# Moving the softmax divisor's small steps from VectorE to ScalarE in a top-k attention and expert kernel

## The chip, the cores and the metric

The kernel runs on one core of a Trainium2 chip. The metric is the device time of one execution in microseconds (us); lower is better. The core has five engines with a queue each, and each queue is worked off in order: TensorE (PE; its weight loads are listed as PEld), VectorE (DVE), ScalarE (ACT), GpSimd (POOL) and SyncE (SP, which here only issues transfers). They meet through semaphores alone.

## The reference

Two blocks follow each other. All data are float32.

```python
# attention: B, H, S, D = 8, 8, 576, 64
scores = q @ k.T / sqrt(D)
kth    = the 32nd largest score of each row
scores = where(scores >= kth, scores, -1e9)
attn   = exp(scores - rowmax)
attn   = attn / (attn.sum(-1) + 1e-09)
x      = (attn @ v) rearranged to (B*S, H*D)          # 4608 x 512
# experts: E = 8, F = 1024
logits = x @ w_gate; e = argmax(logits)
y      = relu(x @ w1[e]) @ w2[e]                      # each row by its own expert
out    = softmax(logits)[e] * y
```

What the change is about is the third last line of the attention block: the row sum of the exponentials, plus 1e-09, by which a row is divided. The kernel multiplies by its reciprocal instead, and does so late, on the finished rows of `x`.

## The kernel before, in words

Two heads of one batch make a *unit*, so there are 32 units (8 batches of 4). A unit has 1152 score rows of 576 keys: nine tiles of 128 rows, four for each head and one shared tail of 64 rows from each. Two tiles are worked on together; nine such pairs cover two neighbouring units, so the main loop `loop()` has 144 passes. In each block of nine passes, pass 0 to 3 belong to the even unit, pass 4 holds the tails of both, and 5 to 8 belong to the odd unit.

One pass goes through the engines like this. TensorE makes the scores (line 276), three passes ahead. ScalarE copies them to SBUF (line 283, tile `s`). VectorE searches each row's 32nd largest score: `fold` (lines 290, 292) and `fold_on` (298, 300) halve the rows, then come rounds of MAX8 (329, 338) and MATCH_REPLACE8 (345). ScalarE scales the threshold (354, tile `low`) and makes a mask by two Relus (370). GpSimd subtracts the mask (379). ScalarE takes the exponentials (387), whose accumulator gives the row sums: one column of the tile `z` (128 x 9, one per unit) for each tile of rows. TensorE transposes the weights (398, 409, 411), ScalarE copies them out of PSUM (402, 404, 417, 419).

When a unit's tiles are done, its end runs in slices spread over later passes. `ending` is a generator that yields the name of the *place* in the pass at which its next slice goes: "small" (behind the search), "relu" (behind the Relus), "products" (at the end of the pass), "rows". The slices are: products with `v` (432), a copy `oT` (434), the second half of both, a turn back with the gate's logits (443), a copy `xl` (450), then GpSimd's scaling by the reciprocals in `logits` (466) and `rows` (479). The reciprocals lie in `rz`, 128 x 10: nine columns as in `z`, and a tenth whose first 64 partitions hold the second head's tail, moved there from partitions 64 to 127 of the ninth. There are two `rz`, for even and odd units.

`divisors` (lines 452 to 459) makes `rz`. It is a generator of VectorE steps, put on the list `aside`; `tick()` takes one step of that list after each MAX8 and MATCH_REPLACE8 of the search from its second round on. So the three small instructions (454 adds epsilon, 456 takes the reciprocal, 458 moves the tenth column) stand between the MAX8s of the next pass's search, in this order: MAX8 (338), 454, MAX8, 456, MATCH_REPLACE8, 458, MATCH_REPLACE8.

The order of instructions on PE, ACT and DVE is that of the program (`manual_schedule`). From the sixth block on, slices of the expert block (`pieces`: lines 663 to 717) are put between, in numbers that the program fixes in advance. What is left of the experts runs after the attention, on TensorE with ScalarE copying out.

Of the kernel before, what the change touches and what calls it, by code (L numbers as in the profile page):

```python
# [11 lines left out]
AF = mybir.ActivationFunctionType  # L12
# [9 lines left out]
EPS = 1e-9  # L22
# [13 lines left out]
def kernel(  # L36
# [46 lines left out]
    nc = tc.nc  # L83
    B, U, P, _ = qk.shape
# [7 lines left out]
    ST = S - SM  # L92
# [5 lines left out]
    NT = 2 * NC + 1  # L98
# [91 lines left out]
    def token_ids(t, b):  # L190
        return nc.gpsimd.iota(t, pattern=[[P, KC]], base=b * S, channel_multiplier=1)

    oT_of, rz_of = [], []
    for n in range(2):
        t = const.tile([P, S if n else KC * P], F32, name=f"oT{n}")
        if not n:
            nc.gpsimd.memset(t[:, S:], 0.0)
        oT_of.append(t)
        t = const.tile([P, NT + 1], F32, name=f"rz{n}")
        nc.gpsimd.memset(t, 0.0)  # L200
        rz_of.append(t)
    wT = const.tile([P, NC, 2, S + ST], F32, name="wT")
    wTt = const.tile([P, S + ST], F32, name="wTt")
# [30 lines left out]
    def in_turn(put):  # L234

        if not k.exact:
            tc.keep_in_program_order(put)
        return put
# [4 lines left out]
    def load_values(n):  # L243
        n.v = k.load.tile([P, KC, P], F32, name="vb")
        nc.sync.dma_start(n.v, v[n.b, n.u, :, :].rearrange("(c p) d -> p c d", p=P))
# [65 lines left out]
    def through(steps):  # L311
        for _ in steps:
            pass
        if steps in aside:
            aside.remove(steps)
# [105 lines left out]
    def outputs(n, x):  # L421

        odd = n.u % 2
        oT = oT_of[odd]
        for j in range(2):
            q = slice(j * HF + (0 if odd else ST), (j + 1) * HF + (0 if odd else ST))
            po = bank("po")
            for c in range(KC):
                for h in range(2):
                    r = slice(h * D, (h + 1) * D)  # L430
                    rhs = wT[:, c, h, q] if c < NC else wTt[:, q]
                    nc.tensor.matmul(po[r, 0:HF], n.v[:, c, r], rhs, start=(c == 0), stop=(c == KC - 1))  # L432
            yield
            nc.scalar.copy(oT[:, j * HF:(j + 1) * HF], po[:, 0:HF])
            yield
        starts = [t * P + (ST if odd else 0) for t in range(NC)] + [0 if odd else SM]
        xw = P + lw
        n.xl = k.small.tile([P, KC, xw], F32, name="xl", bufs=1)
        put = []
        for t0, t1 in ((0, KC - 2), (KC - 2, KC)):  # L440
            px = bank("px")
            for t in range(t0, t1):
                nc.tensor.matmul(
                    px[:, (t - t0) * xw:(t - t0 + 1) * xw], oT[:, starts[t]:starts[t] + P],
                    turn[:, n.u // 2, odd * lw:odd * lw + xw], start=True, stop=True,
                )
            put.append((n.xl[:, t0:t1, :], px[:, 0:(t1 - t0) * xw].rearrange("p (t w) -> p t w", w=xw)))
        yield
        for to, px in put:
            nc.scalar.copy(to, px)  # L450

    def divisors(n):
        rz = rz_of[n.u % 2]
        nc.vector.tensor_scalar_add(rz[:, 0:NT], n.z, EPS)
        yield
        nc.vector.reciprocal(rz[:, 0:NT], rz[:, 0:NT])
        yield
        nc.vector.tensor_copy(rz[0:ST, NT:NT + 1], rz[ST:P, NT - 1:NT])
        yield

    def logits(n, lg):

        rzb = rz_of[n.u % 2][:, :].rearrange("p (t h) -> p t h", h=2)
        at = P if n.u % 2 else 0
        lt = n.xl[:, :, at:at + lw].rearrange("p t (h e) -> p t h e", h=2)
        in_turn(nc.gpsimd.tensor_tensor(lt, lt, _inner(rzb, E), op=ALU.mult))
        if n.u:
            in_turn(nc.gpsimd.tensor_tensor(lg, lg, lt[:, :, 0, :], op=ALU.add))
            in_turn(nc.gpsimd.tensor_tensor(lg, lg, lt[:, :, 1, :], op=ALU.add))
        else:  # L470
            in_turn(nc.gpsimd.tensor_tensor(lg, lt[:, :, 0, :], lt[:, :, 1, :], op=ALU.add))

    def rows(n, x):

        rzb = rz_of[n.u % 2][:, :].rearrange("p (t h) -> p t h", h=2)
        at = 0 if n.u % 2 else lw
        xu = x[:, :, n.u * P:(n.u + 1) * P].rearrange("p t (h d) -> p t h d", h=2)
        xl = n.xl[:, :, at:at + P].rearrange("p t (h d) -> p t h d", h=2)
        in_turn(nc.gpsimd.tensor_tensor(xu, xl, _inner(rzb, D), op=ALU.mult))
# [25 lines left out]
    def ranks(r):  # L505

        rp = bank("rank")
        ohf = r.oh[:, :, :].rearrange("p t e -> p (t e)")
        r.pos, r.run = rp[:, 0:KC * E], rp[:, KC * E:(KC + 1) * E]
        nc.tensor.matmul(rp[:, 0:(KC + 1) * E], ident, _ins(run[:, :], 1, KC + 1), start=True, stop=False)  # L510
        nc.tensor.matmul(r.pos, before, ohf, start=False, stop=False)
        for i in range(1, KC + 1):
            nc.tensor.matmul(
                rp[:, i * E:(KC + 1) * E], ones, ohf[:, 0:(KC + 1 - i) * E], start=False, stop=(i == KC)
            )
# [219 lines left out]
    with fast:  # L735
# [68 lines left out]
        def ending(b, u):  # L804

            nonlocal left
            n = unit[b * U + u]
            if u == 0:
                x_of[b] = k.xp.tile([P, KC, XW], F32, name="x")
                in_turn(token_ids(x_of[b][:, :, Dm + 1].bitcast(I32), b))  # L810
                lg_of[b] = k.small.tile([P, KC, E], F32, name="lg")
            x, lg = x_of[b], lg_of[b]
            out_steps = outputs(n, x)
            yield "products"
            next(out_steps)
            if u % 2 == 0:
                yield "relu"
                next(out_steps)
            yield "small"
            div = divisors(n)  # L820
            aside.append(div)
            if u % 2:
                yield "relu"
                next(out_steps)
            yield "products"
            next(out_steps)
            if b * U + u + 2 < len(units):
                load_values(unit[b * U + u + 2])
            yield "relu"
            next(out_steps)  # L830
            yield "products"
            next(out_steps)
            yield "relu"
            next(out_steps, None)
            yield "rows"
            through(div)
            logits(n, lg)
            rows(n, x)
            if u < U - 1:
                return  # L840
            yield "small"
            r = choice(lg)
            aside.append(r.steps)
            yield "weights"
            yield "turn"
            through(r.steps)
            nc.scalar.activation(lg, lg, AF.Exp)
            yield "products"
            ranks(r)
            yield "small"  # L850
            steps = places(r, x)
            aside.append(steps)
            yield "relu"
            nc.scalar.copy(run, r.run)
            yield "pool"
            through(steps)
            scatters.extend(scattering(r, x))
            if b == B - 1:
                scatter(KC)
                slot_i = k.small.tile([1, 2, NSLOT], I32, name="slot_i")  # L860
                through(table(slot_i, SURE, False))
                firsts = [(slot_i[0:1, 0, j:j + 1], slot_i[0:1, 1, j:j + 1]) for j in range(SURE)]
                ready = load_rows(SimpleNamespace(), firsts[0][1], True)
            new = LAST - SURE if b == B - 1 else new_of[b]
            if new:
                slot_i = slot_last if b == B - 1 else k.small.tile([1, 2, NSLOT], I32, name="slot_i")
                steps = table(slot_i, new, b == B - 1)
                aside.append(steps)
                yield "weights"
                yield "pool"  # L870
                yield "weights"
                yield "pool"
                through(steps)
                coming.extend((slot_i[0:1, 0, j:j + 1], slot_i[0:1, 1, j:j + 1]) for j in range(new))
            if b == B - 1:
                spare.extend(coming[ALWAYS - SURE:])
                del coming[ALWAYS - SURE:]
                assert len(loaded) == 2 and not waiting
                fill_up()
                coming[0:0] = [(firsts[0][0], ready)] + [(expert, (piece,)) for expert, piece in firsts[1:]]  # L880
                scatter(0)
# [125 lines left out]
    with ExitStack() as outer:  # L1007
# [10 lines left out]
        with ExitStack() as st:  # L1018
# [7 lines left out]
            with tc.For_i(0, B, 1) as b:  # L1026
# [3 lines left out]
                for u in range(0, U, 2):  # L1030
# [4 lines left out]
                    for g in groups(u):  # L1035
# [10 lines left out]
                        n, tile = tiles[0]  # L1046
# [76 lines left out]
```

## Time and profile before

| | |
|---|---|
| median of 4 runs | 1374.2 us (1374.14 to 1376.15) |
| the profiled execution, its own time | 1377.23 us |
| its span, first to last instruction | 1375.5 us |
| TensorE clock granted, mean | 0.948 |
| PE busy | 1236.3 us (90%), 7666 instructions |
| DVE busy | 1094.4 us (80%), 4655 |
| ACT busy | 919.7 us (67%), 2049 |
| POOL busy | 647.7 us (47%), 805 |

The busy share is taken over the whole span, which has two stages: the attention with some expert slices up to about 1100 us, in which all four engines work, and the rest of the experts, in which VectorE has almost nothing to do. In the profile a row of the groups names line, engine, operation, tiles and shapes, the count, then busy time and mean duration, then the idle time of that engine just before. A wait is written "engine tile line <- who ended it: us in total, times, longest".

### The profile page before, as it was taken

Reading aid. Unit: us, or ns where it says so; the run is one execution under the profiler, and the core shown is the slowest. Engines: PE = TensorE matmul, PEld = TensorE weight load, DVE = VectorE, ACT = ScalarE, POOL = GpSimd, SP = SyncE. Lnnn points to the kernel's source line nnn. Section 1 sums busy time; section 2 is a strip of 40 time slices with the busy share of each in tenths; the row PEclk is TensorE's granted clock in tenths of the full one; section 3 lists DMA queues with packets and bytes.
Section 4 is the critical chain, followed back from the end, with each engine's and each line's share of the span. In section 5 each row is a group of like instructions: output and inputs, shape, how many; then the busy total and the mean of one; then the engine's idle time right before and its main releaser. Section 6 shows DMA issues by size and latency. Waiting matters only on the chain. (4 is left out here: it accounts for less than half of the span.)

```text
span 1375.5 us, 24487 instructions
## 1 busy us (share of the span) xinstructions
PE 1236.3 (90%) x7666; PEld 839.7 (61%) x7666; DVE 1094.4 (80%) x4655; ACT 919.7 (67%) x2049; POOL 647.7 (47%) x805
## 2 busy tenths in 40 slices
PE   5676777677799999999999999999999999999995
PEld 3344444444466666666766666767676667776773
DVE  8999999999999999999999999999999820000000
ACT  4787778878788888888777788887777821111110
POOL 3454557546645565466555655575556521000000
PEclk9888778788899999999999999999999999999998
DMA  2000011001473357326644474358542759999880
GB/s 82 29 29 29 28 36 55 29 29 36 156 287 137 112 200 289 130 82 241 255 167 174 154 278 154 113 178 304 181 167 83 299 181 356 388 319 333 301 322 18
DMA packets 102220, 231.68 MB, mean 168 GB/s; under 512 B 5182, under 2 KB 25918, under 8 KB 102080
## 3 DMA queue, kind: packets, MB, share of 16 engines
q1 hardware_dynamic: 95328, 209.76, 42.9%
q0 software_dynamic: 6464, 19.97, 4.0%
q8 instruction: 62, 1.02, 0.3%
q14 instruction: 78, 0.64, 0.1%
q10 hardware_dynamic: 288, 0.30, 0.1%
HBM read 208.72 MB, written 22.33 MB: 168 GB/s over the span
## 5 line engine op out<-in xcount | busy, mean ns | idle before, releaser
L379 POOL TENSOR_TENSOR w<-s,w 128x576 f32<-128x576 f32 x288 | 407.3, 1434 | 450.1 <-ACT w L370 449.8
L688 PE MATMUL ph<-xTs,w 128*128 128x128 f32 x2560 | 308.5, 276 | 6.0 <-ACT xTs L665 6.0
L688 PEld LDWEIGHTS ph<-xTs,w 128*128 128x128 f32 x2560 | 297.5, 192 | 26.2 <-issue 18.9
L703 PE MATMUL py<-w,hT 128*128 128x512 f32 x640 | 292.2, 596 | 0.0
L338 DVE MAX8 tops<-scr 128x8 f32<-128x168 f32 x864 | 248.6, 320 | 0.1
L276 PE MATMUL sc<-qkb 64*128 64x288 f32 (+1 forms) x1280 | 222.0, 472 | 9.4 <-ACT s L283 5.2
L387 ACT ACTIVATE w<-w,nbias 128x576 f32<-128x576 f32 x288 | 224.7, 798 | 2.2 <-POOL w L379 2.0
L370 ACT ACTIVATE w<-s,low 128x576 f32<-128x576 f32 x288 | 207.7, 768 | 4.7
L398 PE MATMUL wTm<-turn,w 128*128 128x128 f32 x1152 | 172.9, 291 | 37.8 <-ACT xl L450 25.5
L398 PEld LDWEIGHTS wTm<-turn,w 128*128 128x128 f32 x1152 | 134.7, 148 | 98.5 <-issue 35.4
L1002 DVE CAST any_i<-pd 1x1 int32<-1x1 f32 x1 | 0.1, 147 | 236.0 <-PE pd L1000 236.0
L703 PEld LDWEIGHTS py<-w,hT 128*128 128x128 f32 x640 | 114.4, 190 | 117.6 <-issue 116.5
L345 DVE MATCH_REPLACE8 scr<-tops,scr 128x168 f32<-128x168 f32 x576 | 178.1, 314 | 0.0
L283 ACT COPY s<-sc 128x576 f32<-128x576 f32 x288 | 169.9, 645 | 11.7 <-PE sc L276 11.1
L404 ACT COPY wT<-wTm 128x512 f32<-128x512 f32 x256 | 140.0, 609 | 39.2 <-PE wTm L398 39.0
L276 PEld LDWEIGHTS sc<-qkb 64*128 64x128 f32 (+1 forms) x1280 | 118.3, 195 | 72.8 <-issue 26.4
L432 PE MATMUL po<-wT,vb 128*64 128x288 f32 x1024 | 158.5, 458 | 0.4 <-ACT wTt L419 0.4
L709 POOL DMA_INDIRECT out_dram<-y,xg x40 | 40.6, 1014 | 211.9 <-ACT y L717 199.3
L329 DVE MAX8 few<-l 128x8 f32<-128x288 f32 x288 | 128.0, 445 | 0.0
L432 PEld LDWEIGHTS po<-wT,vb 128*64 128x64 f32 x1024 | 75.5, 152 | 78.6 <-issue 31.1
L693 ACT ACTIVATE hT<-ph 128x512 f32<-128x512 f32 x80 | 48.7, 609 | 108.6 <-PE ph L688 108.5
L290 DVE TENSOR_TENSOR h<-s 128x576 f32<-128x576 f32 x144 | 115.3, 801 | 3.9 <-ACT s L283 3.9
(116 smaller groups left out, 1429.2 us busy)
## 6 DMA issues: line engine op xcount, KB each, us to landing
w<-in_moe_w_dram SPq DMA_DIRECT2D x80, 2048.0 KB, 9.6
qkb<-in_qk_dram SPq DMA_DIRECT2D x31, 608.0 KB, 4.1
xg<-x_rows SPq DMA_DIRECT2D x40, 257.0 KB, 9.8
vb<-in_v_dram SPq DMA_DIRECT2D x32, 320.0 KB, 3.2
x_rows<-blank SPq DMA_DIRECT2D x5, 257.0 KB, 14.2
x_rows<-blank POOLq DMA_DIRECT2D x4, 257.0 KB, 8.7
x_rows<-x,posi POOLq DMA_INDIRECT x40, 3.1
out_dram<-y,xg POOLq DMA_INDIRECT x40, 6.1
```

The source lines that it names most:

```text
L276: nc.tensor.matmul(ps[rows, j, 0:HF], n.q[d, cols], n.k[d, keys], start=True, stop=True)
L283: lambda m=m, ps=ps: nc.scalar.copy(s[:, m, :, :], ps[:, :, 0:HF]) for m, ps in enumerate(got)
L338: nc.vector.max(out=tops[:, m, r * 8:(r + 1) * 8], in_=src[m])
L345: nc.vector.match_replace(out=scr[:, m, :], in_to_replace=tops[:, m, r * 8:(r + 1) * 8], in_values=src[m], imm_value=NEG,)
L370: nc.scalar.activation(w[:, m, :], s[:, m, :, :].rearrange("p j k -> p (j k)"), AF.Relu, scale=-STEEP, bias=low[:, m:m + 1],)
L379: k.last_pool = in_turn(nc.gpsimd.tensor_tensor(w[:, m, :], s[:, m, :, :].rearrange("p j k -> p (j k)"), w[:, m, :], op=ALU.subtract)).ins
L387: nc.scalar.activation(w[:, m, :], w[:, m, :], AF.Exp, scale=scale, bias=nbias[:, m:m + 1], accum_out=n.z[:, c:c + 1])
L398: nc.tensor.transpose(pm[:, c * P:(c + 1) * P], w[:, m, first:first + P], ident)
L404: nc.scalar.copy(wT[:, :, m, q], pm4)
L432: nc.tensor.matmul(po[r, 0:HF], n.v[:, c, r], rhs, start=(c == 0), stop=(c == KC - 1))
L688: nc.tensor.matmul(ph[:, f, :], n.w1[:, 0, dt, fc * P:(fc + 1) * P], n.xT[:, dt, :], start=(dt == 0), stop=(dt == DT - 1),)
L703: nc.tensor.matmul(py, hT[:, f, :], n.w2[:, 0, f, :], start=(f == 0), stop=(f == FT - 1))
```

## The change

`divisors` now gives ScalarE the sum with epsilon and the shifted tenth column, as two activations (a Copy with a constant bias), and VectorE one reciprocal over ten columns. The two activations are issued at once at the place "relu", behind the Relus of the pass (for odd units behind the copy `oT` too, for even units one pass after it); only the reciprocal stays on `aside`. The order of `ending` is changed to fit, and `rz` begins as ones, since the reciprocal now also reads the tenth column's other 64 partitions. On each of the other engines the order of instructions is as before, and so is that of all other instructions on these two.

```diff
-        nc.gpsimd.memset(t, 0.0)
+        nc.gpsimd.memset(t, 1.0)
         rz_of.append(t)
...
     def divisors(n):
         rz = rz_of[n.u % 2]
-        nc.vector.tensor_scalar_add(rz[:, 0:NT], n.z, EPS)
+        nc.scalar.activation(rz[:, 0:NT], n.z, AF.Copy, bias=EPS)
+        nc.scalar.activation(rz[0:ST, NT:NT + 1], n.z[ST:P, NT - 1:NT], AF.Copy, bias=EPS)
         yield
-        nc.vector.reciprocal(rz[:, 0:NT], rz[:, 0:NT])
-        yield
-        nc.vector.tensor_copy(rz[0:ST, NT:NT + 1], rz[ST:P, NT - 1:NT])
+        nc.vector.reciprocal(rz[:, 0:NT + 1], rz[:, 0:NT + 1])
         yield
...
             yield "products"
             next(out_steps)
+            yield "relu"
+            next(out_steps)
             if u % 2 == 0:
                 yield "relu"
-                next(out_steps)
-            yield "small"
             div = divisors(n)
+            next(div)
             aside.append(div)
-            if u % 2:
-                yield "relu"
-                next(out_steps)
             yield "products"
             next(out_steps)
```

## Prediction

> **What bounds the kernel now.** I read the 40 slices of the page first, then the groups with shapes kept apart, the waits, and the timeline around the lines of the change.
>
> ```profile
> PE   5676777677799999999999999999999999999995
> DVE  8999999999999999999999999999999820000000
> ACT  4787778878788888888777788887777821111110
> ```
>
> For 32 slices VectorE is full. TensorE joins it from the twelfth slice and carries the rest alone. So until about 1100 us two engines could be the bound; who waits for whom decides.
>
> ```profile
> DVE h L290 <- ACT s L283: 3.9, 4, 1.3
> ACT low L354 <- DVE tops L338: 87.3, 71, 4.2
> ```
>
> VectorE waited for scores 4 times in 144 passes, 3.9 us in all. ScalarE waited for VectorE's thresholds 71 times, 87.3 us. VectorE sets the pace, and ScalarE, with TensorE behind it, follows. By stretches the second wait is 65.0 us before 400 us, 14.7 us from 400 to 640, none from 640 to 760, 6.9 us from 760 to 920, none from 920 to 1040. In the two stretches with none VectorE itself waited 1.3 us each for scores: there the followers are the bound.
>
> The groups of the change, and two of ScalarE's as prices (busy us, mean ns):
>
> ```profile
> L454 DVE TENSOR_SCALAR rz<-z 128x9 f32<-128x9 f32 x32 | 15.7, 490 | 0.8 <-ACT w L387 0.8
> L456 DVE RECIPROCAL rz<-rz 128x9 f32<-128x9 f32 x32 | 6.2, 193 | 0.0
> L458 DVE COPY rz<-rz 64x1 f32<-64x1 f32 x32 | 4.8, 149 | 0.9
> L354 ACT ACTIVATE low<-tops 128x2 f32<-128x2 f32 x144 | 31.4, 218 | 87.7 <-DVE tops L338 87.3
> L854 ACT COPY run<-rank 128x8 f32<-128x8 f32 x8 | 1.2, 154 | 2.6 <-PE rank L513 2.6
> ```
>
> The sum with epsilon is dear for nine columns: 490 ns in the mean. The view of line 454 gives its spread, and the timeline of unit 19 (units counted from 0) the reason:
>
> ```profile
> L454 DVE TENSOR_SCALAR rz<-z x32: 151/174/1410, 56.8 to 1101.7; 128x9 f32<-128x9 f32 x32
> ```
>
> ```profile
> 683.22 1.44 ACT L370 ACTIVATE w<-s,low 128x576 f32<-128x576 f32 x2
> ...
> 684.08 2.79 POOL L379 TENSOR_TENSOR w<-s,w 128x576 f32<-128x576 f32 x2 [2.44 <-ACT w L370]
> ...
> 684.73 0.79 DVE L454 TENSOR_SCALAR rz<-z 128x9 f32<-128x9 f32 x1
> ...
> 685.43 0.32 DVE L338 MAX8 tops<-scr 128x8 f32<-128x168 f32 x1
> 685.48 0.40 ACT L434 COPY oT<-po 128x288 f32<-128x288 f32 x1 [0.82 <-PE po L432]
> 685.68 0.19 DVE L456 RECIPROCAL rz<-rz 128x9 f32<-128x9 f32 x1
> 685.78 1.19 ACT L283 COPY s<-sc 128x576 f32<-128x576 f32 x2
> ```
>
> GpSimd's first subtraction runs from 684.08 to about 685.49, and 454 ends 30 ns behind it, at 685.52. All thirteen that took over 400 ns end 28 to 35 ns behind such a subtraction: 454 is held until GpSimd is done. The reciprocal isn't: this one began 232 ns into the second subtraction and took 189 ns. Four of the 32 began inside a subtraction (189 to 192 ns); none of the 32 took over 215 ns.
>
> **What goes from VectorE.** The time between the ends of two searches is 7.02 us where nothing stands between (140.41 to 147.43 us) and 7.47 where the three instructions do and none is held (147.43 to 154.90): the three cost 0.45 us, less than their 0.51 of records, which overlap a little. The reciprocal stays, ten columns for nine; by its share (193 of 513 ns) it is 0.17. So 0.28 us go for each unit. The last unit's stand behind the last search, where they set nothing: 31 x 0.28 = 8.7 us. To this come the holds: 15.7 - 32 x 0.174 = 10.1 us. Gross 18.8 us, on an engine that sets the pace.
>
> **What ScalarE gets.** Two activations a unit, 64 in all. The nearest rows are 154 ns (128x8) and 218 ns (128x2); the trace has no 64x1, and line 417's copy, also across partitions, took 253 for 128 columns, which bounds it above. A pair is 0.31 to 0.47 us; I take 0.40, near two of the middle. That is 12.8 us on ScalarE. Where ScalarE then waits for the next threshold they cost nothing, and before 640 us it waits 79.7 us for that against 18 pairs or 7.2 us. If that cover is gone, each pair pushes the copies of the next scores by 0.4 us.
>
> The Trainium skill speaks against this move: its page ScalarE: Activation LUTs, Rules for kernel authors, gives additions to VectorE, as the faster per element. By that rule the addition should stay, and the sum would shrink to the moved column, 32 x 0.149 = 4.8 us. With nine elements no row here is about rate: 174 ns unheld on one engine, 154 to 218 on the other, and the hold is on VectorE's side only; so I go by the rows.
>
> **The new wait.** The reciprocal now waits for the pair. Behind it on VectorE stand the rest of the search, so the threshold, so ScalarE's own next Relus. The pair stands behind the Relus (even units) or `oT` (odd units) of the pass before. The margin is the start of 454 less the end of that instruction; needed are 0.40 for the pair and some 0.05 for the hand-over. In unit 19 it is 684.73 - 685.88 = -1.15 us: VectorE is ahead of ScalarE. Through the 31 units of the loop it is, in us: unit 5 0.45, 7 0.00, 19 -1.15, 21 -0.41, 22 -0.41, 23 0.14, 27 -1.15, 29 -0.40, 30 -0.41, and 1.27 to 4.23 in all others. The stalls are what is missing to 0.45: 0, 0.45, 1.60, 0.86, 0.86, 0.31, 1.60, 0.85, 0.86, together 7.4 us. Seven of these nine units had held 454s (0.79 to 1.41 us), so there one wait takes another's place. GpSimd needs `rz` only a pass or more later (466, 479) and gets it no later than the stall.
>
> Net: 18.8 - 7.4 = 11.4 us. In each of the two stretches with no threshold wait two units stand before VectorE's wait for scores (18 and 19, 26 and 27). They free 0.28 + 0.76 and 0.28 + 0.62 and lose 1.60; the 0.34 left only lengthens that wait. Of their pairs (0.8 us) I count half as pushing scores: 0.74 for each stretch, 1.5 in all. That leaves 9.9 us. The experts' stage keeps its length: the number of slices before it is fixed by the program, so it begins and ends 9.9 us earlier. The profiled execution, 1377.23 (1375.5 of span and 1.7 around it), becomes 1367.3; the median of the runs, 3 us below it, 1374.2 - 9.9 = 1364.3.
>
> What bounds this: with no stall at all 1374.2 - 18.8 = 1355.4. With pairs at 0.47 the eight stalls grow by 0.07 each, 0.6 us in all.
>
> **Rivals.**
> 1. *The wait for ScalarE eats it; slower.* VectorE gets ahead wherever it is freed, ScalarE's lag at the reciprocal grows, and VectorE stalls where it has margin now. The place is the 20 units of the loop from 400 us on. If all stalled like units 19 and 27 (1.60), with 0.45 of unit 7 the stalls were 32.5 and the time 1374.2 - 18.8 + 32.5 = 1387.9; at a mean of 1.2 us, 24.5 and 1379.9. It decides from a mean of (18.8 - 0.45) / 20 = 0.92 us; the margins give 0.35. For it: TensorE is 97 to 99% busy in each stretch of 100 us from 400 to 1000, so the followers have little to catch up with. Against: in 13 of the 20 the margin is 1.27 us or more, and threshold waits of 14.7 and 6.9 us show that ScalarE does catch up.
> 2. *TensorE is the bound from 400 us on.* Then only the first eleven units count: 11 x 0.28, holds of 0.46, 0.32 and 0.57 us, less 0.45: 4.0 us, so 1370.2. Against it stand the same threshold waits.
> 3. *The hold moves with the work.* If the ten-column reciprocal, now first behind the MAX8, is held as 454 was, the 10.1 us stay: 8.7 - 7.4 = 1.3 us, 1372.9. The four reciprocals under a running subtraction speak against it. Line 458's copies began under one four times too, and took 148 to 150 ns. The Trainium skill, in SBUF — State Buffer, Who interferes with whom, names copies, casts and tensor_scalar as VectorE instructions that can wait for GpSimd; by that list the copies should have been held and the reciprocal not, and the sum would be the forecast's.
>
> **Chances.** A measurement of this kernel can tell about 0.2%, 2.7 us. Forecast (5 to 18.8 us faster) 0.62; rival 1 0.20; rival 2 0.13; rival 3 0.05. Faster by over 0.2% are the forecast and most of rival 2, 0.72; within it rival 3 and the rest of rival 2, 0.08; slower 0.20. The range goes from the bound without stalls, 1355.4, up through rivals 2 and 3 into the mild part of rival 1, 1378; what is left out is the rest of rival 1 (0.13) and a few hundredths below.
>
> **What would show it.** Right: VectorE's busy time falls by 15.7 + 4.8 = 20.5 us, but for the holds of other lines; the reciprocal's group stays near 195 ns; VectorE shows a new wait "rz <- ACT rz" of 5 to 9 us, most of it around 680 to 830 and 960 to 1080 us; the last search ends about 10 us before 1095. Each step wrong: a reciprocal of 400 ns and more (hold moved); that wait above 19 us (rival 1); a growing wait of `h` for `s` from 400 us on with the last search little earlier (rival 2); pairs over 0.5 us. If VectorE's tensor_tensor rows (290, 292, 298, 300), which also take longer under GpSimd's subtractions (1.80 us for line 290 at 704.49 us, against 0.74), meet them more often at the new phase, that is a loss I price at nothing; each meeting would cost up to 1 us.

## The result: 1.9 us of the forecast 9.9

The changed kernel takes 1373.1 us (median of 32 runs, 1371.4 to 1374.9) beside 1374.4 us for the kernel before (52 runs). The medians are 1.3 us apart. The ratio over all runs is 0.9986, or 1.9 us, with a 95% interval of 0.9981 to 0.9991: 1.2 to 2.6 us faster, less than a measurement of a few runs would tell from no change. The profiled execution took 1373.76 us, with a span of 1372.2.

### The profile page after: what moved, and what is told of

Its sections match the earlier page's. It is cut to its first block, busy times and chain, and to the rows that moved or that the text cites. A ratio compares the mean times of both kernels' runs of the same rounds, so it can differ in the third digit from the quotient of the medians.

```text
span 1372.2 us, 24487 instructions
## 1 busy us (share of the span) xinstructions
PE 1231.2 (90%) x7666; PEld 838.9 (61%) x7666; DVE 1086.2 (79%) x4591; ACT 930.8 (68%) x2113; POOL 664.7 (48%) x805
## 5 line engine op out<-in xcount | busy, mean ns | idle before, releaser
L338 DVE MAX8 tops<-scr 128x8 f32<-128x168 f32 x864 | 245.8, 316 | 0.0
L432 PE MATMUL po<-wT,vb 128*64 128x288 f32 x1024 | 151.5, 442 | 0.4 <-ACT wTt L419 0.4
## 6 DMA issues: line engine op xcount, KB each, us to landing
xg<-x_rows SPq DMA_DIRECT2D x40, 257.0 KB, 10.1
x_rows<-blank SPq DMA_DIRECT2D x5, 257.0 KB, 14.8
```

The costliest lines, as they stand in the source:

```text
L338: nc.vector.max(out=tops[:, m, r * 8:(r + 1) * 8], in_=src[m])
```

## The profile after

First the waits, in the same form as those of before (us in total, times, longest):

```profile
ACT low L354 <- DVE tops L338: 64.8, 59, 4.2
DVE rz L457 <- ACT rz L455: 10.9, 7, 6.0
DVE h L290 <- ACT s L283: 5.9, 6, 1.6
```

The new wait is there. 6.0 of its 10.9 us belong to the last unit, behind the last search, where they set nothing; 4.9 us lie in the loop, where I had put 7.4. VectorE's wait for scores has grown by 2.0 us.

Then the groups of VectorE and ScalarE with shapes apart (busy us, mean ns, idle before):

```profile
L457 DVE RECIPROCAL rz<-rz 128x10 f32<-128x10 f32 x32 | 6.4, 201 | 11.4 <-ACT rz L455 10.9
L290 DVE TENSOR_TENSOR h<-s 128x576 f32<-128x576 f32 x144 | 117.9, 819 | 5.9 <-ACT s L283 5.9
L300 DVE TENSOR_TENSOR hl<-h 128x288 f32<-128x288 f32 x144 | 69.1, 480 | 0.0
L591 DVE TENSOR_SCALAR ci<-ci 1x8 int32<-1x8 int32 x8 | 4.4, 550 | 0.1
L492 DVE TENSOR_TENSOR oh<-oh,e_less 128x40 f32<-128x40 f32 x8 | 4.2, 528 | 0.0
```
```profile
L454 ACT ACTIVATE rz<-z 128x9 f32<-128x9 f32 x32 | 6.7, 208 | 0.0
L455 ACT ACTIVATE rz<-z 64x1 f32<-64x1 f32 x32 | 6.4, 202 | 0.4
```

The reciprocal is as cheap as hoped and is never held (184 to 218 ns). The pair costs 0.41 us, as taken. But other lines of VectorE have become slower (290, 300, 591 and 492 above). The same lines before the change (591 and 492 were 592 and 493 there):

```profile
L290 DVE TENSOR_TENSOR h<-s 128x576 f32<-128x576 f32 x144 | 115.3, 801 | 3.9 <-ACT s L283 3.9
L300 DVE TENSOR_TENSOR hl<-h 128x288 f32<-128x288 f32 x144 | 67.2, 467 | 0.0
L592 DVE TENSOR_SCALAR ci<-ci 1x8 int32<-1x8 int32 x8 | 1.3, 162 | 0.1
L493 DVE TENSOR_TENSOR oh<-oh,e_less 128x40 f32<-128x40 f32 x8 | 1.5, 187 | 0.0
```

These four alone took back 10.3 us (2.6, 1.9, 3.1 and 2.7). VectorE's busy time in the page fell from 1094.4 to 1086.2 us, by 8.2 where the two removed groups were 20.5. Not every line lost: 298 fell from 77.3 to 76.5 us.

How that comes about is seen around unit 14. The timeline of before, two passes, cut to the lines that matter:

```profile
517.09 2.78 POOL L379 TENSOR_TENSOR w<-s,w 128x576 f32<-128x576 f32 x2 [4.07 <-ACT w L370]
518.95 0.95 DVE L454 TENSOR_SCALAR rz<-z 128x9 f32<-128x9 f32 x1
...
525.18 2.79 POOL L379 TENSOR_TENSOR w<-s,w 128x576 f32<-128x576 f32 x2 [3.67 <-ACT w L370]
...
529.10 0.44 DVE L298 TENSOR_TENSOR few<-h 128x288 f32<-128x288 f32 x1
```

And of after, cut in the same way:

```profile
514.71 2.77 POOL L379 TENSOR_TENSOR w<-s,w 128x576 f32<-128x576 f32 x2 [4.07 <-ACT w L370]
...
515.89 0.20 DVE L457 RECIPROCAL rz<-rz 128x10 f32<-128x10 f32 x1
...
522.94 2.79 POOL L379 TENSOR_TENSOR w<-s,w 128x576 f32<-128x576 f32 x2 [3.80 <-ACT w L370]
...
524.89 1.15 DVE L298 TENSOR_TENSOR few<-h 128x288 f32<-128x288 f32 x1
```

Before, the sum with epsilon was held by the first pair of subtractions, and the next pair had ended 1.1 us before line 298 began. After, the reciprocal passes at once, so that search ends earlier (519.16 us) and ScalarE and GpSimd are further behind it: the next subtractions start 3.78 us after its end, where it was 1.80 before (525.18 - 523.38). VectorE now reaches line 298 while they run, and is held there, 1.15 us for 0.44. It gained 1.15 us in the first of the two passes and gave back 0.71 in the second (search to search: 8.24 to 7.09 us, then 7.02 to 7.73).

To count this over the loop I call *held* what each VectorE instruction took above the lower quartile of its line and shape (the duration that a quarter of them stay under), where that is more than 60 ns. Up to the last search it is 43.6 us before and 44.2 us after. The 10.5 us at line 454 are gone, and as much has appeared elsewhere. That it is GpSimd which holds them shows in the traces: every held instruction of passes 52 to 143, 64 before and 60 after, overlaps one of GpSimd's, and the 17 calls of line 298 that began under a subtraction before all end 0.31 to 0.32 us behind it.

Where along the loop, by the ends of the searches (each eighth MAX8 of line 338 ends a pass; passes 0 to 51 end at 389.49 us before, and unit 10's reciprocals are the last in them):

| us | passes 0 to 51 | passes 52 to 143 | held in 52 to 143 |
|---|---|---|---|
| before | 389.5 | 705.6 | 38.6 |
| after | 385.7 | 707.3 | 39.0 |

The first stretch gained 3.8 us, where my sum had 4.0. The second, in which the expert slices run, lost 1.7, where my sum had a gain of 5.9; the last search ends 2.1 us earlier and not 10. That is the place to look at.

## The experiments

Theory A: from pass 52 on, TensorE with ScalarE behind it sets the pace. Whatever VectorE is freed of there returns as holds and as waits for scores; by this theory holds are for the most part a way in which VectorE waits for the others. Theory B: the gain was real, and the pair on ScalarE with the wait for it ate it.

**No addition, no pair.**

```diff
-        nc.vector.tensor_scalar_add(rz[:, 0:NT], n.z, EPS)
-        yield
-        nc.vector.reciprocal(rz[:, 0:NT], rz[:, 0:NT])
-        yield
-        nc.vector.tensor_copy(rz[0:ST, NT:NT + 1], rz[ST:P, NT - 1:NT])
+        nc.vector.reciprocal(rz[:, 0:NT], n.z)
+        yield
+        nc.vector.reciprocal(rz[0:ST, NT:NT + 1], n.z[ST:P, NT - 1:NT])
```

> The kernel before without the addition of epsilon (the sums are 1 or more, so in float32 it changes nothing): VectorE takes the reciprocal of nine columns straight from z and of the shifted tenth column; ScalarE gets nothing, and the reciprocals wait for nothing new. Theory A (followers): from pass 52 on ScalarE and TensorE set the pace, and what VectorE is freed of there comes back as holds of its other instructions by GpSimd and as waits; only the eleven units before that pay: 11 x 0.15 us + 1.35 us of holds = 3 us, so 1 to 4 us faster. Theory B (the pair): the gain was eaten by ScalarE's two activations and the wait for them; without these it is 31 x 0.15 + 10.1 = 14.7 us, 11 to 15 us faster.

Measured: 0.9995 (0.9986 to 1.0004), no difference that can be told, at or below the lower end of Theory A's 1 to 4 us. Passes 0 to 51 took 387.7 us (1.8 less), passes 52 to 143 704.4 (1.2 less), with 38.3 us held there. The three instructions are cheaper by only 0.06 us where nothing is held (7.48 to 7.42 us for odd units), not by 0.15, but the 10.5 us of holds at line 454 are gone with it. Without any pair and any new wait the gain still isn't there, and the held time is again what it was. Theory B falls.

**The pair alone.**

```diff
+    spare_z = whole[:, 0:NT + 1].bitcast(F32)
...
+    def pair(n):
+        nc.scalar.activation(spare_z[:, 0:NT], n.z, AF.Copy, bias=EPS)
+        nc.scalar.activation(spare_z[0:ST, NT:NT + 1], n.z[ST:P, NT - 1:NT], AF.Copy, bias=EPS)
...
             aside.append(div)
+            yield "relu"
             if u % 2:
-                yield "relu"
                 next(out_steps)
+            pair(n)
```

> The kernel before with ScalarE's two activations added at the place they have in the change, their results written to a scratch tile that nobody reads; VectorE's three instructions stay. The cost of the pair by itself. Theory A (followers set the pace from pass 52 on): 20 pairs of 0.41 us push the scores there, 3 to 9 us slower. If VectorE sets the pace all the way: within 1 us of before. Theory B (the pair ate the gain) needs 8 us or more.

Measured: 1.0017 (1.0008 to 1.0026), 1 to 4 us slower; passes 52 to 143 took 708.4 us, 2.8 more. Some 20 pairs of 0.41 us are 8 us of ScalarE's time, of which a third shows. Passes 0 to 51 took 388.5 us, 1.0 less though work was added, so a difference of about 1 us in the first stretch of one profile says nothing.

**Less work for TensorE**, with the kernel before and with the changed one.

```diff
-                for dt in range(DT):
+                for dt in range(DT // 2):
                     nc.tensor.matmul(
                         ph[:, f, :], n.w1[:, 0, dt, fc * P:(fc + 1) * P], n.xT[:, dt, :],
-                        start=(dt == 0), stop=(dt == DT - 1),
+                        start=(dt == 0), stop=(dt == DT // 2 - 1),
                     )
```

> The kernel before with half of the expert block's first product left out (two of four steps of its contraction), so that TensorE has some 12 us less work in each 100 us from 400 us on; the outputs of the experts are not the reference's. Serves as the base for light_after. Theory A: VectorE's waits and holds from pass 52 on shrink, and the last search ends 15 us or more earlier than before's; in all some 80 us faster, mostly from the last stage.

> The changed kernel with the same half of the expert block's first product left out. To be read against light_before. Theory A (followers set the pace from pass 52 on, because TensorE has no slack): with TensorE relieved the change brings what was forecast, 8 to 12 us. Theory B (ScalarE's pair and the wait for it): 1 to 4 us, as with the full experts. If the holds only fall anew by the chance of their phase: anywhere between 0 and 12 us, with the total held time again equal.

Measured: 1313.7 us and 1300.6 us, 0.9548 (0.9536 to 0.9560) and 0.9456 (0.9443 to 0.9468) of before. With TensorE relieved the same edit brings 13.1 us, somewhat more than the 8 to 12 expected. The base kernel gained 62 us where I had expected 80, and its last search ends 23.8 us earlier, all of it from passes 52 to 143 (705.6 to 681.5 us). By stretches the change takes it from 389.7 to 385.4 us in passes 0 to 51 and from 681.5 to 671.9 in the rest. The base kernel's waits show that VectorE sets the pace now, 131.9 us where it was 87.3 (in passes 52 to 143 alone 66.9 for 22.3):

```profile
ACT low L354 <- DVE tops L338: 131.9, 120, 4.2
```

The groups, of the light kernel before the change and of the light changed one:

```profile
L298 DVE TENSOR_TENSOR few<-h 128x288 f32<-128x288 f32 x144 | 70.0, 486 | 0.0
L454 DVE TENSOR_SCALAR rz<-z 128x9 f32<-128x9 f32 x32 | 6.7, 210 | 1.1 <-ACT w L387 1.1
```
```profile
L298 DVE TENSOR_TENSOR few<-h 128x288 f32<-128x288 f32 x144 | 71.5, 496 | 0.0
L457 DVE RECIPROCAL rz<-rz 128x10 f32<-128x10 f32 x32 | 6.2, 193 | 6.2 <-ACT rz L455 6.2
```

Even line 454 is hardly held now (210 ns in the mean, not 490): the subtractions come early enough in the search to miss it. Held time in passes 52 to 143 is 16.9 and 14.8 us. The light changed kernel has one wait for the pair, that of the last unit; in the loop none. Most units gain 0.35 to 0.40 us from search to search (7.48 to 7.09 us for odd units).

**Less work for VectorE.**

```diff
-TOP_K = 32
+TOP_K = 24
```

> The kernel before with three rounds of the search for four (the 24 largest scores are kept, not 32), so that VectorE has about 1.4 us less in each of the 144 passes; the outputs are those of a top 24. What ScalarE and TensorE need by themselves, with VectorE well ahead. Theory A (followers set the pace from pass 52 on): passes 52 to 143 take nearly what they take before, 705.6 us, that is 690 us or more, and VectorE waits for scores by 100 us and more. If VectorE sets the pace there, holds included: some 92 x 1.4 = 129 us less, 577 to 620 us.

Measured, in two runs: 1333.95 us, 0.9703 (0.9686 to 0.9721). Passes 0 to 51 took 349.1 us, 40.4 less. Passes 52 to 143 took 700.8, 4.8 less, though VectorE had some 99 us less to do there: a pass in which nothing is held takes 5.94 us for 7.02, so that 1.08 us went from each and not the 1.4 expected. Its groups and its wait for scores:

```profile
L290 DVE TENSOR_TENSOR h<-s 128x576 f32<-128x576 f32 x144 | 116.0, 806 | 26.9 <-ACT s L283 26.4
L300 DVE TENSOR_TENSOR hl<-h 128x288 f32<-128x288 f32 x144 | 98.4, 683 | 0.0
L298 DVE TENSOR_TENSOR few<-h 128x288 f32<-128x288 f32 x144 | 94.5, 657 | 0.0
```

Held time in that stretch rises from 38.6 to some 95 us (90 to 99, by how the quartile of groups of a few instructions is taken), and the wait for scores from 3.9 to 26.4 us in the whole loop. Of these two channels the hold is the larger. So 700.8 us is about what the others need, and an edit of VectorE alone could have won about those 4.8 us there and little more. I had expected waits of 100 us and more, and not that holds would stand for most of them.

**The change in parts**: the first eleven units alone, and the others alone (there the comparison is >=). The diff is against the changed kernel; the places in `ending` follow the same test.

```diff
+EARLY = 11
...
+    def on_scalar(n):
+        return n.b * U + n.u < EARLY
...
+        if k.exact or not on_scalar(n):
+            nc.vector.tensor_scalar_add(rz[:, 0:NT], n.z, EPS)
+            yield
+            nc.vector.reciprocal(rz[:, 0:NT], rz[:, 0:NT])
+            yield
+            nc.vector.tensor_copy(rz[0:ST, NT:NT + 1], rz[ST:P, NT - 1:NT])
+            yield
+            return
```

> The change in the first eleven units alone; from unit 11 on the steps of the kernel before. Theory A: all that the change gains lies there, passes 0 to 51 are 3.8 us shorter, and the time 3 to 4.5 us lower. If the gain were spread over the units: a third of the change's own, 0.5 to 1 us.

> The change from unit 11 on alone; the first eleven units as in the kernel before. Theory A: no gain, and ScalarE's pairs are pushed onto a bound chain: 0 to 3 us slower. The forecast's own sum for these units: 20 x 0.28 + 8.8 of holds - 6.9 of stalls - 1.5 = 6 us faster.

Measured: 0.9983 (0.9974 to 0.9992) and 1.0007 (0.9998 to 1.0016). The eleven early units carry the whole gain (passes 0 to 51: 385.8 us; the rest 705.1). That is 1.1 to 3.6 us by the times, where 3 to 4.5 were expected. The 21 late ones bring nothing, and by the trace cost 1.0 us (706.6 for 705.6). The loss is small but comes again: passes 52 to 143 took 705.6 and 705.1 us in the two profiles with the late units as before, and 707.3, 707.3 and 706.6 in the three with the change there.

**A version made of both**, again against the changed kernel: the pair for the early units, and for the late ones two reciprocals straight from `z`.

```diff
+        if k.exact or n.b * U + n.u >= EARLY:
+            yield
+            nc.vector.reciprocal(rz[:, 0:NT], n.z)
+            yield
+            nc.vector.reciprocal(rz[0:ST, NT:NT + 1], n.z[ST:P, NT - 1:NT])
+            yield
+            return
         nc.scalar.activation(rz[:, 0:NT], n.z, AF.Copy, bias=EPS)
```

> A version that may beat both: the change in the first eleven units, where VectorE sets the pace; from unit 11 on nothing for ScalarE, and VectorE takes two reciprocals straight from z (the addition of epsilon to sums of 1 or more is left out, which in float32 changes nothing). Theory A: 3.8 us from passes 0 to 51 and 0 to 1.5 us from the rest, 3.5 to 5.5 us faster than before. Theory B (the pair and its wait ate the gain): 3.8 + 9 or more, 11 to 15 us.

Measured: 1370.35 us, 0.9972 (0.9962 to 0.9982), 3.9 us faster than before; passes 52 to 143 took 704.3 us. Once more, beside the changed kernel:

> The changed kernel once more, on the same chip as the next one. From the 32 runs: 0.1 to 0.2% below before.

> The split version once more, beside the changed kernel. Theory A: 2 to 3 us below it (the 1.7 us that the change loses from pass 52 on, and about 1 us that the split version gains there).

Measured: 0.9989 (0.9980 to 0.9998) for the changed kernel and 0.9982 (0.9973 to 0.9992) for this one. The stretch from pass 52 on came out the same as in the first runs (707.3 and 704.2 us), while passes 0 to 51 of this version differed by 1.2 us (384.5 and 385.8). The medians lie 1.2 us apart, where 2 to 3 were expected, and the intervals of the whole time overlap: it beats the kernel before, and whether it beats the changed kernel isn't settled by the times.

## Why the prediction was wrong, point by point

- *What bounds the kernel.* This step failed: "VectorE sets the pace, and ScalarE, with TensorE behind it, follows" holds for passes 0 to 51 only. I took VectorE's small idle time as proof. But its busy time from pass 52 on had 38.6 us in it in which GpSimd stood in its way, and the short search shows that these stretch to fit: some 95 us when VectorE has less to do. I had found the hold at line 454 and read it as a cost of that instruction, so I counted 10.1 us of holds as gain. It was a wait for the late subtractions, and those were late because TensorE was: with TensorE relieved the same line takes 210 ns and not 490. In place of the 5.9 us of gain from pass 52 on the runs show a loss of 1.7.
- *The threshold waits.* I brought them (14.7 and 6.9 us) as the reason against rival 2, TensorE as the bound from 400 us on. They come in 25 of the 92 passes from pass 52 on, 19 of these without any hold, and 42 others have holds and no such wait. So ScalarE does catch up now and then, but that is no slack of the stretch: it became only 4.8 us shorter when VectorE was freed of some 99. What decides in which passes they fall isn't shown. Rival 2 had the mechanism, and its 1370.2 us lies nearer to the measured 1373.1 than my 1364.3; its sign came too, if small (the wait for scores from pass 52 on grew from 2.5 to 4.0 us). What it lacked is the pair: from pass 52 on ScalarE's work is on the bound chain, and the change loses 1.7 us there.
- *Two-input instructions under the subtractions.* My last paragraph named lines 290, 292, 298 and 300 and priced them "at nothing". Three of them lost: 2.6 us (290), 1.3 (292) and 1.9 (300). Line 298 did as a whole not, though single calls did, as behind unit 14. With four small lines (591, 492, 607 and 611: 9.6 us), and less some 3.6 us that two others gained, the rest of VectorE took back about as much as line 454 had lost.
- *The early units.* 4.0 us forecast, 3.8 measured, which is partly luck: the eleven passes themselves gained 5.4 us, and three others (12, 17 and 27) gave back 1.5 as holds at lines 298 and 292. The unit's own saving was sized too low: the reciprocal costs 0.07 us from search to search (7.09 against 7.02), not 0.17, so 0.35 to 0.40 us went for each unit and not 0.28. With TensorE relieved, that and the holds come to about the 13.1 us of the light kernels.
- *The pair, the wait, the hold.* The pair at 0.41 us (0.40 taken) and the reciprocal that is never held are as forecast; the wait came to 4.9 us in the loop (7.4 taken). Rival 1 (the wait eats the gain) and rival 3 (the hold moves to the reciprocal) did not come; the hold moved, but to other lines.

The Trainium skill's rule that gives additions to VectorE (ScalarE: Activation LUTs, Rules for kernel authors), for its rate per element in bf16, decided nothing here: with few elements the pair took 208 and 202 ns against 163 and 149 ns unheld on VectorE, and the place in the loop, not the engine's rate, settled whether that mattered. The same skill's page SBUF — State Buffer, Who interferes with whom, also says that a VectorE instruction with two SBUF inputs contends with a GpSimd instruction that reads SBUF. That agrees with line 298 at 1.15 us under the subtraction and 0.44 us clear of it. Its list of copies, casts and tensor_scalar, which rival 3 quotes, says only that they can contend, under conditions on their operands; so the four copies that were not held do not speak against it.

## What to carry to other kernels

A busy share near 100% does not make an engine the bound: compare its instructions' mean with their shortest form, and look at who runs beside them when they take longer; that difference can be waiting. To find which of two full engines sets the pace, relieve one generously in a kernel whose output does not matter; the short search and the light kernels took one edit each and settled it here. A saving on one engine is worth what the stage allows in which it falls, so place it by stage.

## What the runs showed of the hardware

I had not expected holds to regulate the pace so finely: held time in the loop stayed at 42 to 45 us in all kernels with the full experts and the full search, whichever VectorE instructions were taken out. Small instructions were held as long as large ones: line 492 (128x40) took 528 ns in the mean against 187 before, three of its eight having met a subtraction (1.09 us each). VectorE's reciprocal was never held (184 to 218 ns in the changed kernel, 189 to 215 before), though 24 of its 32 calls in the changed kernel began under a subtraction. And a meeting does not always hold VectorE: in the changed kernel two calls of line 298 and four of line 300 began under a subtraction and took 435 to 450 ns, and there the subtraction itself took 1.8 to 2.3 us in place of 1.4.
